# Chunked attention into a two-layer feed-forward block: VectorE's half of a step emitted one step later, squares of batch 0 moved to GpSimd, and first-layer matmuls pulled into the attention's tail

## The chip, the cores and the metric

The kernel runs on one core of a Trainium2 chip. The metric is device time in microseconds (us) of one execution, lower is better. The kernel before took 244.06 us as the median of 8 runs, 242.99 to 246.07.

## The reference

Four batches, eight heads, 768 rows, head size 64. Attention runs in chunks of 32 rows; each chunk sees 8 memory rows, 16 rows to the left of it and 8 to the right. The heads' outputs, side by side, are the 512 columns of `x`, and a feed-forward block with a sine in the middle follows (`alpha` is one number for each of 2048 hidden columns):

```python
scores = scale * np.matmul(q_c, k_full.transpose(0, 1, 3, 2))
a = np.exp(scores - max); a = a / (np.sum(a, axis=-1, keepdims=True) + 1e-09)
out[:, :, c_start:c_end] = np.matmul(a, v_full)
...
h = x @ w_in                             # 3072 x 512 by 512 x 2048
s = np.sin(alpha * h)
g = h + s * s / (alpha + 1e-09)
return (g @ w_out).astype(np.float32)    # 3072 x 2048 by 2048 x 512
```

## The kernel before, in words

All five engines run their own instructions in the order in which the program emits them (`manual_schedule`); no scheduler reorders them. What sets the order of the work is therefore the order of the code, and an engine that waits holds up everything behind it in its queue.

**Per batch** the kernel does four things.

- *Transposes.* Eight "pieces" (`t_k`, `t_q`; four pairs of heads, key and query). A piece copies heads together into `pr` (L226, VectorE, ScalarE or GpSimd), transposes it on TensorE (L242 for keys, L257 for queries) into a PSUM tile `tt`, and copies that out: keys to `kTi` on VectorE (L243 and two small L249), queries to `qT` on ScalarE (L258).
- *Attention* (`burst`), in 8 blocks of 96 rows: scores `sc` (L266), three Exp on ScalarE (L275), P·V into `ot` (L288), reciprocal and scaling on VectorE (L292, L293), transposes (L306), and a copy of `x` transposed to `xT` on VectorE (L309). In batch 0, `spin` (L171) adds matmuls on zeros.
- *First layer* (`l1`), 16 steps (`ft` 0 to 15). A step is 8 matmuls into `hT`, 128 x 2 x 384 in two PSUM banks (L341), one sine on ScalarE (`u`, L353), the square of the sine (`s2`; on ScalarE L356, on VectorE or GpSimd L358, as the string at L460 says with A, D or P), and one VectorE instruction that scales, adds `hT` and writes `gT` (L367). In batch 0, steps 3, 7 and 11 use the two small PSUM banks (`hs`) instead, with two half-width sines (L350) and two half-width VectorE instructions (L363).
- *Second layer* (`l2`), six times 16 matmuls into `o` (L393), a copy to `o_sb` (L400 on VectorE, L402 on ScalarE in turn) and a store (L403). It is a generator; `Stream.take(n)` emits its next n matmuls as filler between the steps of the following batch. If a block of 16 ends within a take, its `o_sb` copy is emitted there, and the take stops.

**PSUM**: `big` holds three tiles of two banks (`sc`, `ot`, `hT`, and `tt_b` in part), `smp` two of one bank (`o`, `z`, `hs`, `xtp`, and `tt_a`). A step's matmuls thus need the `hT` tile of three steps before, which L367 has to have read. In batches 1 and 2, one piece is emitted before every even step, and its `tt_a` shares the two small banks with `o`.

**Order around the change.** In a step of batches 1 to 3 the code emits: `take` (filler; perhaps an `o_sb` copy), a piece at even steps, then `l1` with matmuls, sine, square and L367. So on VectorE, L367 of one step stands ahead of the `o_sb` and `kTi` copies of the next.

**Loads** of weights, keys, queries and values go through GpSimd's DMA queue (L102 to L151, L212, L218); GpSimd issues them in order, and each waits for the load eight places ahead of it, whose semaphore it takes over. For batch 0's first layer the order is: 8 pieces of `w_in` (256 columns each, two steps' worth), keys and queries of batch 1, 4 pieces of `w_out` (four steps' worth each), and 4 loads of values for batch 1. The memory values of all batches are cast once on ScalarE (`memv_st`, L413), and broadcast per batch by VectorE (`put_memv`, L153).

Of the kernel before, what the change touches and what calls it, by code (L numbers as in the profile page):

```python
# [9 lines left out]
P = 128  # L10
QW = 96
# [34 lines left out]
def kernel(  # L46
# [12 lines left out]
    nc = tc.nc  # L59
    B, H, S, D = q.shape  # L60
# [16 lines left out]
    big = ctx.enter_context(tc.tile_pool(name="big", bufs=3, space=bass.MemoryType.PSUM))  # L77
    smp = ctx.enter_context(tc.tile_pool(name="smp", bufs=2, space=bass.MemoryType.PSUM))
# [129 lines left out]
    for pt in pts:  # L208
        nc.vector.memset(pt[:, H * QW:H * QW + 32], 0.0)

    def load_w_in(c):
        nc.gpsimd.dma_start(  # L212
            w_in_sb[:, :, 256 * c:256 * c + 256],
            moe_w_in[:, 256 * c:256 * c + 256].rearrange("(kt p) f -> p kt f", p=P),
        )
# [84 lines left out]
    def xt(xT, j, x_blk, ot):  # L300
        if ot is None:
            xtp = smp.tile([P, KT, QW], BF, name="xtp", tag="sm")[:]
        else:
            xtp = ot[:].bitcast(BF)[:, 0, 640:640 + KT * QW].rearrange("p (k c) -> p k c", k=KT)
        for kt in range(KT):
            nc.tensor.transpose(  # L306
                xtp[:, kt, :], x_blk[:, 2 * kt:2 * kt + 2, :].rearrange("p e d -> p (e d)"), ident[0:QW, 0:QW]
            )
        nc.vector.tensor_copy(xT[:, :, QW * j:QW * j + QW], xtp)  # L309

    def burst(b, stream, shares, lag):
# [21 lines left out]
    def l1(i, ft, xT, gT, sq, split=False):  # L333
        if split:
            hts = [smp.tile([P, 512], F32, name="hs", tag="sm") for _ in range(2)]
        else:
            hT = big.tile([P, 2, 512], F32, name="hT", tag="big")
            hts = [hT[:, 0], hT[:, 1]]
        for kt in range(KT):
            for hf in range(2):  # L340
                nc.tensor.matmul(  # L341
                    hts[hf][:, 0:HALF],
                    w_in_sb[:, kt, P * ft:P * ft + P],
                    xT[:, kt, HALF * hf:HALF * hf + HALF],
                    start=(kt == 0), stop=(kt == KT - 1),
                )
        u = mlp.tile([P, 2, HALF], F32, name="u")
        if split:
            for hf in range(2):
                nc.scalar.activation(  # L350
                    u[:, hf], hts[hf][:, 0:HALF], ACTF.Sin, scale=alpha_sb[:, ft:ft + 1])
        else:
            nc.scalar.activation(u[:], hT[:, :, 0:HALF], ACTF.Sin, scale=alpha_sb[:, ft:ft + 1])  # L353
        s2 = mlp.tile([P, 2, HALF], F32, name="s2")
        if sq == "A":
            nc.scalar.activation(s2[:], u[:], ACTF.Square)  # L356
        else:
            (nc.vector if sq == "D" else nc.gpsimd).tensor_tensor(  # L358
                out=s2[:], in0=u[:], in1=u[:], op=ALU.mult)
        gv = gT[:, ft, :].rearrange("p (e c) -> p e c", e=2)  # L360
        for hf in range(2):
            if split:
                nc.vector.scalar_tensor_tensor(  # L363
                    out=gv[:, hf], in0=s2[:, hf], scalar=inv_alpha[:, ft:ft + 1],
                    in1=hts[hf][:, 0:HALF], op0=ALU.mult, op1=ALU.add)
            elif hf == 0:
                nc.vector.scalar_tensor_tensor(  # L367
                    out=gv, in0=s2[:], scalar=inv_alpha[:, ft:ft + 1],
                    in1=hT[:, :, 0:HALF], op0=ALU.mult, op1=ALU.add)
# [39 lines left out]
    for n in range(2 * HP):  # L409
        (t_k if n % 2 == 0 else t_q)(prs[n], n // 2)  # L410
        spin(2)
        if n == 3:
            nc.scalar.copy(memv_st[64:72], memv_f[64:72])  # L413
# [105 lines left out]
```

## Time and profile before

| | |
|---|---|
| median of 8 runs | 244.06 us |
| the profiled execution | 243.94 us |
| its span, first to last instruction | 241.7 us |
| TensorE busy | 217.2 us (90%) |
| VectorE busy | 161.0 us (67%) |
| ScalarE busy | 154.6 us (64%) |
| GpSimd busy | 73.4 us (30%) |
| granted TensorE clock | 1.000 |

The stages, by the first and last instruction of each on TensorE: attention of batch 0 to 27.8 us; its first layer to 51.6; transposes of batch 1 to 61.7; attention of batch 1 to 80.3; first layer 1 to 112.5; attention 2 to 134.1; first layer 2 to 167.3; attention 3 to 189.2; first layer 3 to 217.2; and the last second layer to the end.

How to read the rows that follow: a row of a timeline has the start and the length in us, the engine, the line, the operation, what it writes and reads, and how many instructions were merged; in brackets stands how long the engine was idle before and what ended that. Engines: PE is TensorE (PEld its weight loads), DVE VectorE, ACT ScalarE, POOL GpSimd, SP the queue of the stores. A row of the waits has who waited for whom, then the total in us, how often, and the longest. TensorE's lengths include the drain of the array, so rows overlap: eight first-layer matmuls follow each other in 1.30 us.

### The profile page before, as it was taken

Reading aid. Unit: us, or ns where it says so; the run is one execution under the profiler, and the core shown is the slowest. Engines: PE = TensorE matmul, PEld = TensorE weight load, DVE = VectorE, ACT = ScalarE, POOL = GpSimd, SP = SyncE. Lnnn points to the kernel's source line nnn. Section 1 sums busy time; section 2 is a strip of 40 time slices with the busy share of each in tenths; the row PEclk is TensorE's granted clock in tenths of the full one; section 3 lists DMA queues with packets and bytes.
Section 4 is the critical chain, followed back from the end, with each engine's and each line's share of the span. In section 5 each row is a group of like instructions: output and inputs, shape, how many; then the busy total and the mean of one; then the engine's idle time right before and its main releaser. Section 6 shows DMA issues by size and latency. Waiting matters only on the chain.

```text
span 241.7 us, 4472 instructions
## 1 busy us (share of the span) xinstructions
PE 217.2 (90%) x1759; PEld 121.7 (50%) x1785; DVE 161.0 (67%) x287; ACT 154.6 (64%) x237; POOL 73.4 (30%) x96
## 2 busy tenths in 40 slices
PE   6688899978989989898999996998999999899994
PEld 2346465535445555454455653554455555453453
DVE  3578979999268667969557686968557267876100
ACT  3599499963884467788564775778764775871000
POOL 8899855423912114147210214120000001020000
PEclk9999999999999999999999999999999999999999
DMA  7999999999999810109994101001111101101122
GB/s 81 164 118 88 150 189 204 207 205 136 180 216 152 86 46 0 44 1 160 164 148 88 46 0 43 3 0 43 46 43 47 43 0 46 43 0 43 43 90 87
DMA packets 53852, 21.11 MB, mean 87 GB/s; under 512 B 36296, under 2 KB 50888, under 8 KB 53832
## 3 DMA queue, kind: packets, MB, share of 16 engines
q0 software_dynamic: 47616, 14.40, 70.1%
q1 hardware_dynamic: 6216, 6.43, 9.0%
q8 instruction: 14, 0.23, 0.4%
q14 instruction: 6, 0.05, 0.1%
HBM read 28.91 MB, written 6.29 MB: 146 GB/s over the span
## 4 chain that ended last, share of the span: by engine, by line
PE 43%; DMA 15%; DVE 13%; issue 11%; POOL 9%; ACT 7%; POOLq 1%; DVEq 0%; ACTq 0%
PE o L393 25%; DMA w_out_sb<-in_moe_w_out_dram 8%; PE hT L341 8%; DVE gT L367 6%; DVE s L358 4%; DMA w_in_sb<-in_moe_w_in_dram 4%; POOL vw L129 3%; ACT u L353 3%; PE ot L288 3%; POOL s L358 2%; PE sc L266 2%; DMA q_bf<-in_q_dram 2%; POOL vw L125 2%; ACT s L356 2%; ACT pt L275 2%
## 5 line engine op out<-in xcount | busy, mean ns | idle before, releaser
L393 PE MATMUL o<-w_out_sb,gT 128*128 128x512 bf16 x343 | 93.4, 380 | 2.8 <-DMA w_out_sb<-in_moe_w_out_dram 0.8
L341 PE MATMUL hT<-xT,w_in_sb 128*128 128x384 bf16 x488 | 87.5, 326 | 4.5 <-DVE gT L367 4.1
L367 DVE SCALAR_TENSOR_TENSOR gT<-s,inv_alpha,hT 128x768 bf16<-128x768 f32 x61 | 61.2, 1012 | 28.5 <-ACT s L356 20.0
L353 ACT ACTIVATE u<-hT,alpha_sb 128x768 f32<-128x768 f32 x61 | 54.7, 898 | 27.2 <-PE hT L341 26.0
L341 PEld LDWEIGHTS <-w_in_sb 128*128 128x128 bf16 x512 | 49.3, 98 | 39.3 <-issue 6.4
L275 ACT ACTIVATE pt<-sc,biasm 128x256 bf16<-128x256 f32 x96 | 37.6, 493 | 13.0 <-PE sc L266 13.0
L393 PEld LDWEIGHTS <-gT 128*128 128x128 bf16 x368 | 31.8, 98 | 26.4 <-DVE gT L367 1.4
L358 POOL TENSOR_TENSOR s<-u 128x768 f32<-128x768 f32 x6 | 8.8, 1466 | 73.7 <-ACT u L353 73.7
L356 ACT ACTIVATE s<-u 128x768 f32<-128x768 f32 x34 | 28.7, 843 | 1.1
L358 DVE TENSOR_TENSOR s<-u 128x768 f32<-128x768 f32 x24 | 25.2, 1049 | 0.4 <-ACT u L353 0.3
L226 POOL COPY pr<-q_bf 128x768 bf16<-128x768 bf16 x12 | 10.8, 901 | 40.0 <-PE tt_a L242 25.2
L293 DVE TENSOR_TENSOR x_blk<-ot,rinv 96x512 bf16<-96x512 f32 x32 | 22.0, 686 | 1.1
L292 DVE RECIPROCAL rinv<-ot 96x8 f32<-96x8 f32 x32 | 6.4, 201 | 20.1 <-PE ot L288 19.8
L402 ACT COPY o_sb<-o 128x512 f32<-128x512 f32 x11 | 6.4, 586 | 20.0 <-PE o L393 20.0
L400 DVE COPY o_sb<-o 128x512 f32<-128x512 f32 x12 | 8.3, 689 | 15.9 <-PE o L393 15.9
L288 PEld LDWEIGHTS <-pt 128*128 128x128 bf16 x256 | 11.9, 97 | 7.2 <-issue 2.3
L288 PE MATMUL ot<-vw,pt 128*128 128x65 bf16 x256 | 13.0, 193 | 0.9 <-ACT pt L275 0.6
L171 PE MATMUL z<-zeros 128*128 128x512 bf16 x36 | 12.5, 426 | 1.5 <-DVE zeros L165 1.3
L266 PEld LDWEIGHTS <-kTi 64*128 64x128 bf16 x256 | 6.9, 94 | 12.8 <-issue 6.4
L257 PEld LDWEIGHTS <-pr 128*128 128x128 bf16 x96 | 6.3, 97 | 13.7 <-issue 7.8
L266 PE MATMUL sc<-qT,kTi 64*128 64x96 bf16 x256 | 11.3, 205 | 1.8 <-ACT pt L275 1.2
L306 PEld LDWEIGHTS <-x_blk 96*128 96x128 bf16 x128 | 8.4, 97 | 6.6 <-DVE x_blk L293 1.5
(66 smaller groups left out, 180.8 us busy)
## 6 DMA issues: line engine op xcount, KB each, us to landing
out_dram<-o_sb SPq DMA_DIRECT2D x23, 256.0 KB, 2.2
k_bf<-in_k_dram POOLq DMA_DIRECT2D x3, 768.0 KB, 9.1
q_bf<-in_q_dram POOLq DMA_DIRECT2D x3, 768.0 KB, 12.8
vw<-in_v_dram POOLq DMA_DIRECT2D x6, 384.0 KB, 17.1
w_in_sb<-in_moe_w_in_dram POOLq DMA_DIRECT2D x8, 256.0 KB, 8.7
w_out_sb<-in_moe_w_out_dram POOLq DMA_DIRECT2D x4, 512.0 KB, 18.5
k_bf<-in_k_dram POOLq DMA_DIRECT2D x4, 192.0 KB, 5.7
q_bf<-in_q_dram POOLq DMA_DIRECT2D x4, 192.0 KB, 6.0
```

Source lines behind the costliest of these rows:

```text
L171: nc.tensor.matmul(z[:], zeros[:, 0:P], zeros[:])
L226: (eng or nc.gpsimd.tensor_copy)(pr[:].rearrange("p r e d -> p e r d"), src[:, 2 * hp:2 * hp + 2])
L266: nc.tensor.matmul(sc[:, e, QW * hp:QW * hp + QW], kTi[64 * e:64 * e + 64, hp, 104 * j:104 * j + P], qT[64 * e:64 * e + 64, hp, QW * j:QW ...
L275: nc.scalar.activation(pt[:, 0:H * QW].rearrange("p (g e c) -> p e g c", g=4, e=2)[:, :, :, 32 * m:32 * m + 32], sc[:, :, 0:4 * QW].rearra ...
L288: nc.tensor.matmul(otv[:, h // 4, h % 4, :], pt[:, QW * h:QW * h + P], vws[b % 2][:, h, j, 0:D + 1])
L293: nc.vector.tensor_tensor(out=x_blk[:].rearrange("p (g e) d -> p g e d", g=2), in0=otv[0:QW, :, :, 0:D], in1=rv.unsqueeze(3).to_broadcast( ...
L341: nc.tensor.matmul(hts[hf][:, 0:HALF], w_in_sb[:, kt, P * ft:P * ft + P], xT[:, kt, HALF * hf:HALF * hf + HALF], start=(kt == 0), stop=(kt ...
L353: nc.scalar.activation(u[:], hT[:, :, 0:HALF], ACTF.Sin, scale=alpha_sb[:, ft:ft + 1])
L356: nc.scalar.activation(s2[:], u[:], ACTF.Square)
L358: (nc.vector if sq == "D" else nc.gpsimd).tensor_tensor(out=s2[:], in0=u[:], in1=u[:], op=ALU.mult)
L367: nc.vector.scalar_tensor_tensor(out=gv, in0=s2[:], scalar=inv_alpha[:, ft:ft + 1], in1=hT[:, :, 0:HALF], op0=ALU.mult, op1=ALU.add)
L393: nc.tensor.matmul(o[:], gT[:, ft, P * s:P * s + P], w_out_sb[:, ft, :], start=(ft == 0), stop=(ft == FT - 1),)
```

## The change

It has five parts.

1. **The lag.** `l1` now returns a function `finish` with VectorE's part of the step (a square marked D, L372, and L380, which was L367; halves L376). It is called after the next step's `take` and piece, and before the next step's matmuls.
2. **Batch 0's squares**: the string goes from 10 A and 6 D to 8 A, 4 D and 4 P (steps 6, 8, 10 and 12 on GpSimd).
3. **Batch 0's attention tail**: the last three copies to `xT` go to ScalarE; the first-half matmuls (columns 0 to 383) of steps 0 and 1 are emitted at the last-but-one turn of the burst, behind P·V of block 7 and behind the transposes of block 6; the cast of `memv_st` does batch 0 at its old place and the other three batches after the burst.
4. **Fewer weight loads**: `w_in` in 5 (256, 256, 512, 512, 512 columns) instead of 8, `w_out` in 2 instead of 4.
5. **Last batch**: 2 instead of 3 second-layer matmuls per step.

```diff
-    def load_w_in(c):
+    def load_w_in(c0, c1):
...
-            w_out_sb[:, 4 * c:4 * c + 4, :],
+            w_out_sb[:, 8 * c:8 * c + 8, :],
...
-        nc.vector.tensor_copy(xT[:, :, QW * j:QW * j + QW], xtp)
+        (nc.scalar.copy if ot is None and j >= 5 else nc.vector.tensor_copy)(
+            xT[:, :, QW * j:QW * j + QW], xtp)
...
+            if hook:
+                hook(s, 0, xT)
             stream.take((n + 1) // 3, True)
             if 0 <= s - lag - 1 < NJ:
                 xt(xT, s - lag - 1, *xbl.pop(s - lag - 1))
+            if hook:
+                hook(s, 1, xT)
...
+    def l1_mm(hts, ft, xT, kt, hf):
+        nc.tensor.matmul(
+            hts[hf][:, 0:HALF],
+            w_in_sb[:, kt, P * ft:P * ft + P],
+            xT[:, kt, HALF * hf:HALF * hf + HALF],
+            start=(kt == 0), stop=(kt == KT - 1),
+        )
...
+        elif sq == "P":
+            nc.gpsimd.tensor_tensor(out=s2[:], in0=u[:], in1=u[:], op=ALU.mult)
+
+        def finish():
+            if sq == "D":
+                nc.vector.tensor_tensor(out=s2[:], in0=u[:], in1=u[:], op=ALU.mult)
...
+                elif hf == 0:
+                    nc.vector.scalar_tensor_tensor(
+                        out=gv, in0=s2[:], scalar=inv_alpha[:, ft:ft + 1],
+                        in1=hT[:, :, 0:HALF], op0=ALU.mult, op1=ALU.add)
+
+        return finish
...
-            nc.scalar.copy(memv_st[64:72], memv_f[64:72])
+            nc.scalar.copy(memv_st[64:72, 0], memv_f[64:72, 0])
...
-    for c in range(8):
-        load_w_in(c)
+    for c0, c1 in ((0, 256), (256, 512), (512, 1024), (1024, 1536), (1536, 2048)):
+        load_w_in(c0, c1)
...
+    def early(s, point, xT):
+
+        ft = {(9, 0): 0, (9, 1): 1}.get((s, point))
+        if ft is not None:
+            opened[ft] = l1_open(ft)
+            for kt in range(KT):
+                l1_mm(opened[ft], ft, xT, kt, 0)
+
+    xT = burst(0, stream, (), 2, early)
+    nc.scalar.copy(memv_st[64:72, 1:B], memv_f[64:72, 1:B])
...
-            sq = ("ADADADAAADADADAA" if i == 0 else "ADAAPDADADAPADAD")[ft]
+            sq = ("ADADAAPDPAPAPDAA" if i == 0 else "ADAAPDADADAPADAD")[ft]
             if 1 <= ft:
-                stream.take(3 if last else 2)
+                stream.take(2)
...
+            if finish is not None:
+                finish()
+            split = i == 0 and ft in (3, 7, 11)
+            if ft in opened:
+                finish = l1(ft, xT, gT, sq, opened.pop(ft), (1,))
+            else:
+                finish = l1(ft, xT, gT, sq, l1_open(ft, split), (0, 1), split)
+        finish()
```

Where this moves instructions. ScalarE, from the last Exp of batch 0's attention to the first square, before:

```order
L275 ACTIVATE pt_94<-sc,biasm 128x2x4x32 x3
L353 ACT_TABLE_LOAD
L353 ACTIVATE u<-hT,alpha_sb 128x768
L356 ACTIVATE s_619<-u 128x768
L353 ACTIVATE u<-hT,alpha_sb 128x768 x2
```

and now:

```order
L275 ACTIVATE pt_94<-sc,biasm 128x2x4x32 x3
L309 COPY xT<-xtp 128x4x96 x3
L462 CAST memv_st<-memv_f 8x1536
L363 ACT_TABLE_LOAD
L363 ACTIVATE u<-hT,alpha_sb 128x768
L366 ACTIVATE s_620<-u 128x768
```

Three copies and the larger part of the cast have come in front of the sine's table load and the first sine. VectorE, first layer of batch 1 from its start to step 4, before:

```order
L243 COPY kTi<-tt_a 128x7x96
L249 COPY kTi<-tt_a 128x48 x2
L367 SCALAR_TENSOR_TENSOR gT<-s_1304,inv_alpha,hT 128x768
L400 COPY o_sb<-o 128x512
L358 TENSOR_TENSOR s_1322<-u 128x768
L367 SCALAR_TENSOR_TENSOR gT<-s_1322,inv_alpha,hT 128x768
L367 SCALAR_TENSOR_TENSOR gT<-s_1350,inv_alpha,hT 128x768
L367 SCALAR_TENSOR_TENSOR gT<-s_1366,inv_alpha,hT 128x768
L243 COPY kTi<-tt_a 128x7x96
L249 COPY kTi<-tt_a 128x48 x2
```

and now:

```order
L243 COPY kTi<-tt_a 128x7x96
L249 COPY kTi<-tt_a 128x48 x2
L415 COPY o_sb<-o 128x512
L380 SCALAR_TENSOR_TENSOR gT<-s_1300,inv_alpha,hT 128x768
L372 TENSOR_TENSOR s_1318<-u 128x768
L380 SCALAR_TENSOR_TENSOR gT<-s_1318,inv_alpha,hT 128x768
L380 SCALAR_TENSOR_TENSOR gT<-s_1346,inv_alpha,hT 128x768
L243 COPY kTi<-tt_a 128x7x96
L249 COPY kTi<-tt_a 128x48 x2
L380 SCALAR_TENSOR_TENSOR gT<-s_1362,inv_alpha,hT 128x768
```

The copy to `o_sb` has moved ahead of step 0's L380, and the key copies ahead of step 3's. GpSimd, from the first piece of `w_in` to its first own work, before:

```order
L212 DMA w_in_sb<-in_moe_w_in_dram 128x4x256 x8
L115 DMA k_bf<-in_k_dram 128x8x384
L115 DMA q_bf<-in_q_dram 128x8x384
L218 DMA w_out_sb<-in_moe_w_out_dram 128x4x512 x4
L139 DMA vw_86<-in_v_dram 48x64x64
L142 DMA vw_86<-in_v_dram 48x64x64
L145 DMA vw_86<-in_v_dram 16x63x64
L148 DMA vw_86<-in_v_dram 8x63x64
L226 COPY pr<-q_bf 128x2x6x64 x4
```

and now:

```order
L212 DMA w_in_sb<-in_moe_w_in_dram 128x4x256 x2
L212 DMA w_in_sb<-in_moe_w_in_dram 128x4x512 x3
L115 DMA k_bf<-in_k_dram 128x8x384
L115 DMA q_bf<-in_q_dram 128x8x384
L218 DMA w_out_sb<-in_moe_w_out_dram 128x8x512 x2
L139 DMA vw_86<-in_v_dram 48x64x64
L142 DMA vw_86<-in_v_dram 48x64x64
L145 DMA vw_86<-in_v_dram 16x63x64
L148 DMA vw_86<-in_v_dram 8x63x64
L368 TENSOR_TENSOR s_702<-u 128x768
L368 TENSOR_TENSOR s_733<-u 128x768
L368 TENSOR_TENSOR s_761<-u 128x768
```

Thirteen loads stand there instead of eighteen, and behind them the squares of steps 6, 8 and 10 (and, further on, 12) ahead of the query copies.

More of the change, by code (lines that the diff above doesn't have):

```diff
@@ L209 @@
         nc.vector.memset(pt[:, H * QW:H * QW + 32], 0.0)
-    def load_w_in(c):
+    def load_w_in(c0, c1):
         nc.gpsimd.dma_start(
-            w_in_sb[:, :, 256 * c:256 * c + 256],
-            moe_w_in[:, 256 * c:256 * c + 256].rearrange("(kt p) f -> p kt f", p=P),
+            w_in_sb[:, :, c0:c1],
+            moe_w_in[:, c0:c1].rearrange("(kt p) f -> p kt f", p=P),
         )
@@ L308, in xt, with burst @@
             )
[L309 to L311 removed]
+        (nc.scalar.copy if ot is None and j >= 5 else nc.vector.tensor_copy)(
+            xT[:, :, QW * j:QW * j + QW], xtp)
+    def burst(b, stream, shares, lag, hook=None):
         xT = xp.tile([P, KT, S], BF, name="xT")
@@ L328, in burst, with l1_open, l1 @@
                 xt(xT, s - lag - 1, *xbl.pop(s - lag - 1))
+            if hook:
+                hook(s, 1, xT)
             stream.take((n + 2) // 3, True)
         return xT
-    def l1(i, ft, xT, gT, sq, split=False):
+    def l1_open(ft, split=False):
         if split:
[L335 to L338, printed above, removed]
-        for kt in range(KT):
[L340 to L346, printed above, removed]
+            return [smp.tile([P, 512], F32, name="hs", tag="sm") for _ in range(2)]
+        hT = big.tile([P, 2, 512], F32, name="hT", tag="big")
+        return [hT[:, 0], hT[:, 1], hT]
+    def l1_mm(hts, ft, xT, kt, hf):
[5 more added lines that the diff above has]
+        )
+    def l1(ft, xT, gT, sq, hts, halves, split=False):
+        for kt in range(KT):
+            for hf in halves:
+                l1_mm(hts, ft, xT, kt, hf)
+        hT = None if split else hts[2]
         u = mlp.tile([P, 2, HALF], F32, name="u")
@@ L356, in l1 @@
             nc.scalar.activation(s2[:], u[:], ACTF.Square)
[L357 to L369, printed above, removed]
+        elif sq == "P":
[3 more added lines that the diff above has]
+                nc.vector.tensor_tensor(out=s2[:], in0=u[:], in1=u[:], op=ALU.mult)
+            gv = gT[:, ft, :].rearrange("p (e c) -> p e c", e=2)
+            for hf in range(2):
+                if split:
+                    nc.vector.scalar_tensor_tensor(
+                        out=gv[:, hf], in0=s2[:, hf], scalar=inv_alpha[:, ft:ft + 1],
+                        in1=hts[hf][:, 0:HALF], op0=ALU.mult, op1=ALU.add)
+                elif hf == 0:
+                    nc.vector.scalar_tensor_tensor(
+                        out=gv, in0=s2[:], scalar=inv_alpha[:, ft:ft + 1],
+                        in1=hT[:, :, 0:HALF], op0=ALU.mult, op1=ALU.add)
+        return finish
     def l2(i, gT, last=False):
@@ L427 @@
     nc.vector.reciprocal(inv_alpha[:], alpha_sb[:])
-    for c in range(8):
-        load_w_in(c)
+    for c0, c1 in ((0, 256), (256, 512), (512, 1024), (1024, 1536), (1536, 2048)):
+        load_w_in(c0, c1)
     kq_next = load_qk(1)
-    for c in range(4):
+    for c in range(2):
         load_w_out(c)
```

6 lines of the change are left out of this document (3 added, 3 removed).

## The prediction

> **What bounds the kernel now.** I began with the busy time in the three stages that the change touches most: batch 0's first layer, then the first layers of batches 1 and 2 (columns: span, then busy time of PE, PEld, DVE, ACT, POOL).
>
> ```profile
> 27.80:51.60 23.80, 21.47 (x132) 12.47 (x129) 21.41 (x27) 20.35 (x27) 11.15 (x12) 1.00 1.32 196
> 80.30:112.50 32.20, 28.25 (x193) 16.91 (x194) 24.60 (x34) 23.72 (x29) 12.03 (x12) 1.00 0.21 39
> 134.10:167.30 33.20, 29.75 (x202) 17.48 (x205) 24.91 (x33) 23.55 (x29) 7.12 (x7) 1.00 0.07 25
> ```
>
> Batch 0 has three engines near their limit at once: VectorE 21.4 and ScalarE 20.4 of 23.8 us. In batches 1 and 2 only TensorE is full, and the granted clock is 1.00. What TensorE does not use there is what can be won. So the second view is TensorE's waits, for batches 1, 2 and 3 in turn:
>
> ```profile
> PE tt_a L257 <- DVE o_sb L400: 1.4, 1, 1.4
> PE hT L341 <- DVE gT L367: 1.0, 2, 0.5
> PE tt_a L257 <- DVE kTi L249: 1.0, 1, 1.0
> PE sc L266 <- DVE gT L367: 0.5, 1, 0.5
> ```
>
> ```profile
> PE tt_a L257 <- DVE o_sb L400: 1.7, 1, 1.7
> PE tt_a L257 <- DVE kTi L249: 1.4, 2, 0.9
> ```
>
> ```profile
> PE hT L341 <- DVE gT L367: 1.1, 2, 0.9
> PE o L393 <- DVE gT L367: 0.4, 1, 0.4
> ```
>
> That is 3.9, 3.1 and 1.5 us, every one of them on VectorE. The largest, in batch 2, row by row (GpSimd, VectorE, TensorE):
>
> ```profile
> 144.54 1.46 POOL L358 TENSOR_TENSOR s<-u 128x768 f32<-128x768 f32 x1 [5.16 <-ACT u L353]
> ```
>
> ```profile
> 146.03 1.01 DVE L367 SCALAR_TENSOR_TENSOR gT<-s,inv_alpha,hT 128x768 bf16<-128x768 f32 x1 [0.73 <-POOL s L358]
> 146.96 0.68 DVE L400 COPY o_sb<-o 128x512 f32<-128x512 f32 x1
> 147.56 0.95 DVE L358 TENSOR_TENSOR s<-u 128x768 f32<-128x768 f32 x1
> ```
>
> ```profile
> 147.70 0.49 PE L257 MATMUL tt_a<-ident,pr 128*128 128x128 bf16 x6 [1.73 <-DVE o_sb L400]
> ```
>
> VectorE stood idle 0.73 us in front of L367, for GpSimd's square. The evacuation L400 was queued behind it, and TensorE waited 1.73 us for the bank that L400 frees. It is waiting in line, not work.
>
> **The lag, batches 1 and 2.** `finish` puts L400, L243 and L249 ahead of the square and L367 of the step before. In the case shown the copy would run ahead of L367 and end before TensorE asks for the bank, so the 1.73 goes; likewise the other waits on `o_sb` and `kTi`, 1.4 + 1.0 and 1.7 + 1.4 = 5.5 us in all. The price is that L367, which frees the `hT` bank, comes after a key evacuation:
>
> ```profile
> 163.00 0.85 DVE L243 COPY kTi<-tt_a 128x672 bf16<-128x672 bf16 x1
> 163.77 0.31 DVE L249 COPY kTi<-tt_a 128x48 bf16<-128x48 bf16 x2
> ```
>
> ```profile
> 25.08 1.28 ACT L353 ACT_TABLE_LOAD   x1
> 29.73 0.90 ACT L353 ACTIVATE u<-hT,alpha_sb 128x768 f32<-128x768 f32 x1 [3.36 <-PE hT L341]
> 30.66 0.84 ACT L356 ACTIVATE s<-u 128x768 f32<-128x768 f32 x1
> 31.41 0.88 ACT L353 ACTIVATE u<-hT,alpha_sb 128x768 f32<-128x768 f32 x1
> ```
>
> ```profile
> 189.21 1.30 PE hT L341 x8
> ```
>
> A step's bank is needed again three steps on. With two second-layer matmuls (0.43) in each step and the transposes (0.34) in every second, that is two steps of 1.73 plus 0.77 = 4.2 us after its own matmuls end. Sine 0.90, square 0.84 to 0.95, L367 1.01 and handovers take 3.0. So 1.2 us is to spare, and one evacuation costs 0.85 + 0.31 = 1.16. It just fits. I charge 0.1 for each of the four key pieces: batch 2 gains 3.1 - 0.4 = 2.7. In batch 1 the second-layer matmuls run out after step 9; from there the loop is two steps of 1.30 plus 0.34 = 2.9, which is under 3.0, so half of the 1.5 us of waits for L367 (`hT` and `sc`) stays: 3.9 - 0.4 - 0.8 = 2.7. Bounds for the two together: none of it (the waits move to `hT`) up to all 7.0.
>
> **Last batch, two instead of three matmuls per step.** 26 second-layer matmuls are left there. At three a step they are gone by step 9, and the tail runs at 1.30 a step, where the 0.9 and 0.27 of waits lie. At two a step they last to step 13 at 1.73 a step, so those 1.1 us go. Against it: the last two steps are still bare (0.1), and the last `o_sb` copy on ScalarE falls in front of the last sines (I take 0.2 of its 0.6). Together -0.8; bounds 0 and -1.5.
>
> **Batch 0, when the first sine starts.** Rows of the end of its attention, of the first `w_in` piece and of the `memv_st` cast:
>
> ```profile
> 25.87 0.40 PE L288 MATMUL ot<-vw,pt 128*128 128x65 bf16 x8
> 26.50 0.34 PE L306 MATMUL xtp<-ident,x_blk 96*128 96x96 bf16 x4 [0.22 <-DVE x_blk L293]
> ```
>
> ```profile
> 22.34 5.98 POOL L212 DMA_DIRECT2D w_in_sb<-in_moe_w_in_dram  x8
> ```
>
> ```profile
> w_in_sb<-in_moe_w_in_dram POOLq DMA_DIRECT2D x1, 256.0 KB, 4.3
> ```
>
> ```profile
> 12.30 1.90 ACT L413 CAST memv_st<-memv_f 8x2048 bf16<-8x2048 f32 x1
> ```
>
> ```profile
> 27.46 0.34 DVE L309 COPY xT<-xtp 128x384 bf16<-128x384 bf16 x1
> ```
>
> ```profile
> 28.49 1.76 DVE L153 COPY vw<-memv_st 8x4096 bf16<-8x4096 bf16 x1
> ```
>
> The early matmuls stand in TensorE's queue behind 25.87 + 0.40 = 26.27 and need the first `w_in` piece, which lands at 22.34 + 4.3 = 26.64. So TensorE, which today goes straight on, waits 0.4 with the transposes of blocks 6 and 7 behind it. Then four matmuls (half of 1.30) to 27.3, transposes to 27.6, four matmuls to 28.3, the filler 0.2, and the last transposes to 28.8. ScalarE's copy of the last block: between VectorE's 0.34 and the 0.84 that ScalarE's square of twice the columns takes, I take 0.5, to 29.3. Then, new in this place, three quarters of the cast: 1.4, to 30.7. Then the table load, which before was hidden behind the attention's end: 1.28, to 32.0. The first sine was at 29.73, so ScalarE starts 2.3 us later. L153 on VectorE, which waits for the cast, runs from 30.7 to 32.5 and is covered: VectorE has nothing else until the first square ends at 33.7. The eight early matmuls win nothing, since TensorE does not hold up ScalarE here. VectorE's three copies (0.34 each) and the split of the cast win nothing either: the first cast at 12.30 only delays query copies that wait for their load anyway.
>
> **Batch 0, squares on GpSimd.** By the rows of 29.73 to 31.41 a sine with a ScalarE square takes 1.68, a sine alone 0.92. With 8 squares instead of 10, ScalarE alone would be through at 32.0 + 8 x 1.68 + 8 x 0.92 = 52.8. But a GpSimd square takes 1.46 against 0.84, and VectorE stands in line for it. Followed step by step: sine 6 ends at 41.5, its square at 43.0, while VectorE has been free since 41.7. The square of step 8 runs from 43.4 to 44.9 and meets VectorE's square of step 7. What that costs is in batch 1:
>
> ```profile
> 94.46 0.82 POOL L226 COPY pr<-k_bf 128x768 bf16<-128x768 bf16 x1
> 94.71 1.38 DVE L358 TENSOR_TENSOR s<-u 128x768 f32<-128x768 f32 x1
> ```
>
> VectorE's square took 1.38 instead of 0.95 and ended 0.81 after GpSimd's copy ended: it hardly ran beside it. So step 7's square ends at 45.7, its two L376 at 46.9. Only then can step 11 use both small banks, so its sine starts at 48.1. Sine 12 ends at 50.8, its GpSimd square at 52.4, its L380 at 53.4; step 15's matmuls need that bank and end at 54.75; sine, square and L380 end at 57.8. Against before:
>
> ```profile
> 52.71 1.93 DVE L367 SCALAR_TENSOR_TENSOR gT<-s,inv_alpha,hT 128x768 bf16<-128x768 f32 x2
> 54.56 0.85 DVE L243 COPY kTi<-tt_b 128x672 bf16<-128x672 bf16 x1
> ```
>
> ```profile
> 56.45 0.38 PE L393 MATMUL o<-w_out_sb,gT 128*128 128x512 bf16 x1 [0.77 <-DMA w_out_sb<-in_moe_w_out_dram]
> ```
>
> There L367 ended at 54.6, so VectorE reaches batch 1's key copies 3.1 us later. Part comes back: the wait of 0.77 for `w_out` is behind by then. Batch 0: +2.3. Bounds: -0.4 (VectorE starts 2.3 later, saves two squares of 0.95, never waits for GpSimd, and the 0.77 goes) and +3.4 (nothing comes back, ScalarE's copies at 0.84).
>
> Here a page bears on it: the Trainium skill, "SBUF — State Buffer", section "Who interferes with whom", says that a VectorE instruction with two SBUF inputs and a GpSimd instruction that reads SBUF exclude each other, the second waiting for the whole of the first. It speaks against putting squares on both engines in turn. The row at 94.71 agrees with it, ending 0.81 after GpSimd. If the two merely slowed each other in proportion, step 7 would lose 0.4 instead of 0.8, and the sum would be 0.4 lower.
>
> **Fewer weight DMAs.** The bytes and their order on the queue stay. Halved `w_out` means that step 8 of the second layer, not step 12, needs the last piece. It landed at 56.4; TensorE now comes to step 8 at 57.6, so it is covered. If batch 0 were not late, TensorE would wait there from 54.5, up to 1.9 us. For GpSimd the gain is needed by its squares. Before, it was held by the loads until here:
>
> ```profile
> 46.42 0.83 POOL L148 DMA_DIRECT2D vw<-in_v_dram  x1 [3.13 <-DMA q_bf<-in_q_dram]
> 47.25 1.59 POOL L226 COPY pr<-q_bf 128x768 bf16<-128x768 bf16 x1
> ```
>
> ```profile
> vw<-in_v_dram POOLq DMA_DIRECT2D x1, 63.0 KB, 18.8
> ```
>
> Each load waits for the one eight places ahead of it; with 13 loads instead of 18 the last `v` waits for the last `w_in` piece, not for `q`. All `w_in` pieces were issued by 28.3 and are ahead of `k` and `q` in the queue, so I take GpSimd as free at about 39, before its first square at 41.5. The last `v` landed at 46.42 + 18.8 = 65.2, and batch 1's first P·V needs it; 2 us later it no longer matters, but it keeps batch 0 from gaining more than about half a microsecond.
>
> **The sum.** The profiled execution took 243.94 us (span 241.7); the median of the eight is 244.06, 0.1 above. 243.94 + 2.3 - 2.7 - 2.7 - 0.8 = 240.0; against the median 240.1.
>
> **Rivals.**
> 1. Batch 0 comes out even: the later sine is made good by fewer squares on ScalarE and VectorE. For it: both are at 86 to 90% there. Against: the chain through steps 6, 8, 11, 12 and 15. 240.1 - 2.3 = 237.8. Chance 0.15.
> 2. Half of the lag's 5.4 us comes back as waits for `hT`, since 1.2 us of slack against 1.16 leaves nothing for a square held up by GpSimd: 240.1 + 2.7 = 242.8. Chance 0.18, half of it on either side of 0.5%.
> 3. Slower: GpSimd is still issuing loads when its first square is due. The row at 46.42 shows it held to 47.25; from 41.5 on every microsecond counts one for one, up to 5.7. Against: the lanes above. 240.1 + 5.7 = 245.8. Chance 0.06.
> 4. Slower: each of eight key pieces holds back L380 by its full 1.16, with TensorE waiting on `hT`: 240.1 + 5.4 - 5.5 + 9.3 = 249.3. Decides where the slack is under zero; against it is the 4.2 us. Chance 0.06.
>
> **How the numbers follow.** My forecast has 0.55, as 238.4 to 241.8. 0.5% (1.2 us) is about what a measurement can tell from no change. Faster: 0.55 + 0.15 + 0.09 = 0.79; within: 0.09; slower: 0.12. The range reaches from below rival 1 (237.0) to just over rival 2 (243.2), leaving out rivals 3 and 4 and the ends.
>
> **What would show it.** Right: first sine near 32.0; VectorE's square of step 7 about 1.7 long or late; first Exp of batch 1 (63.24 before, below) about 2.3 later; no `o_sb` or `kTi` wait of TensorE in batches 1 and 2, and those stages 2.7 us shorter; the last batch without the 0.9 wait.
>
> ```profile
> 63.24 1.20 ACT L275 ACTIVATE pt<-sc,biasm 128x256 bf16<-128x256 f32 x3
> ```
>
> Wrong: first Exp at or before 63.24 (rival 1), new waits of `hT` on L380 of over 1 us a batch (2, 4), GpSimd's first square well after 42 (3).

## The result, and the profile after

The changed kernel takes **239.09 us** (median of 11 runs, 238.07 to 240.33). The ratio to the kernel before, from the fast runs of both in one set, is 0.9764, with a 95% interval of 0.9735 to 0.9794, so it is 2.4% faster; against the 244.06 above, which is from other runs, it is 5.0 us or 2.0%. The forecast was 240.1, with a range of 237.0 to 243.2. The profiled execution took 238.53 us, with a span of 236.7 (before 243.94 and 241.7).

The quickest way to cut both spans into stages is ScalarE's table loads, which mark each change between Exp and sine. Before (L275 loads for Exp, L353 for sine; the first row is the 24 Exp of batch 0's attention, which end at 25.06):

```profile
16.13 8.93 ACT L275 ACTIVATE pt<-sc,biasm 128x256 bf16<-128x256 f32 x24 [0.37 <-PE sc L266]
...
61.95 1.28 ACT L275 ACT_TABLE_LOAD   x1
77.54 1.28 ACT L353 ACT_TABLE_LOAD   x1
112.97 1.28 ACT L275 ACT_TABLE_LOAD   x1
133.45 1.28 ACT L353 ACT_TABLE_LOAD   x1
168.71 1.28 ACT L275 ACT_TABLE_LOAD   x1
188.38 1.28 ACT L353 ACT_TABLE_LOAD   x1
```

After (sine is L363 now):

```profile
16.63 8.92 ACT L275 ACTIVATE pt<-sc,biasm 128x256 bf16<-128x256 f32 x24 [0.37 <-PE sc L266]
...
64.86 1.28 ACT L275 ACT_TABLE_LOAD   x1
80.45 1.28 ACT L363 ACT_TABLE_LOAD   x1
113.37 1.28 ACT L275 ACT_TABLE_LOAD   x1
133.05 1.28 ACT L363 ACT_TABLE_LOAD   x1
164.57 1.28 ACT L275 ACT_TABLE_LOAD   x1
184.47 1.28 ACT L363 ACT_TABLE_LOAD   x1
```

| stage | before | after | difference |
|---|---|---|---|
| start to the last Exp of batch 0 (untouched but for a shorter cast) | 25.06 | 25.55 | +0.5 |
| from there to batch 1's load for Exp (first layer of batch 0, transposes) | 36.89 | 39.31 | +2.4 |
| attention of batch 1, to the load for sine | 15.59 | 15.59 | 0 |
| from there to batch 3's load for sine (first layers of batches 1 and 2, attentions of 2 and 3) | 110.84 | 104.02 | -6.8 |
| from there to the end of the span | 53.3 | 52.2 | -1.1 |

So the gain lies where the lag acts, the last batch adds a little, and batch 0 gives back a third; e1 and e2 below take the lag apart from the rest. TensorE's share in the two lagged stages (columns: span, busy PE, PEld, DVE, ACT, POOL, then granted clock, DMA share and GB/s), each taken from batch 1's or 2's first matmul of the first layer to that of the next batch. Before:

```profile
80.69:134.46 53.77, 49.42 (x421) 28.11 (x426) 38.46 (x64) 37.16 (x57) 15.48 (x16) 1.00 0.83 77
134.46:189.05 54.59, 50.73 (x422) 28.29 (x427) 38.06 (x62) 37.23 (x58) 7.12 (x7) 1.00 0.08 29
```

After:

```profile
83.60:134.05 50.45, 49.12 (x421) 28.24 (x426) 38.87 (x64) 36.78 (x57) 15.42 (x16) 1.00 0.81 81
134.05:185.13 51.08, 49.96 (x421) 28.60 (x427) 38.02 (x62) 36.79 (x58) 7.01 (x7) 1.00 0.08 31
```

TensorE stood idle 4.35 and 3.86 us before, 1.33 and 1.12 after. What is left of its waits on VectorE, in batches 1, 2 and 3 in turn:

```profile
PE hT L345 <- DVE gT L380: 0.7, 2, 0.5
...
PE sc L266 <- DVE gT L380: 0.6, 1, 0.6
...
PE o L408 <- DVE gT L380: 0.4, 1, 0.4
```

The waits on `o_sb` and `kTi` are all gone, as forecast, and so is the 0.9 in the last batch.

The head of batch 0's first layer, on ScalarE: three copies, the cast, then the table load, which is followed by the first sine:

```profile
26.28 0.48 ACT L309 COPY xT<-xtp 128x384 bf16<-128x384 bf16 x1 [0.72 <-PE xtp L306]
27.76 0.48 ACT L309 COPY xT<-xtp 128x384 bf16<-128x384 bf16 x1 [1.00 <-PE xtp L306]
28.80 0.48 ACT L309 COPY xT<-xtp 128x384 bf16<-128x384 bf16 x1 [0.56 <-PE xtp L306]
29.30 1.47 ACT L462 CAST memv_st<-memv_f 8x1536 bf16<-8x1536 f32 x1
30.79 1.28 ACT L363 ACT_TABLE_LOAD   x1
32.09 0.90 ACT L363 ACTIVATE u<-hT,alpha_sb 128x768 f32<-128x768 f32 x1
```

And the place where squares of both engines meet, VectorE first, then GpSimd:

```profile
42.97 1.01 DVE L380 SCALAR_TENSOR_TENSOR gT<-s,inv_alpha,hT 128x768 bf16<-128x768 f32 x1 [1.26 <-POOL s L368]
43.90 1.97 DVE L372 TENSOR_TENSOR s<-u 128x768 f32<-128x768 f32 x1
45.91 1.14 DVE L376 SCALAR_TENSOR_TENSOR gT<-s,inv_alpha,hs 128x384 bf16<-128x384 f32 x2
...
43.59 1.47 POOL L368 TENSOR_TENSOR s<-u 128x768 f32<-128x768 f32 x1 [0.65 <-ACT u L363]
```

VectorE waits for GpSimd's square of step 6 (1.26), then its own square of step 7 takes 1.97 and ends 0.81 after GpSimd's.

### The profile page after: what moved, and what is told of

The parts are those of the page before. It is cut to its first block, busy times and chain, and to the rows that moved or that the text cites. A ratio compares the mean times of both kernels' runs of the same rounds, so it can differ in the third digit from the quotient of the medians.

```text
span 236.7 us, 4468 instructions
## 1 busy us (share of the span) xinstructions
PE 217.0 (92%) x1759; PEld 122.3 (52%) x1785; DVE 158.7 (67%) x282; ACT 154.1 (65%) x239; POOL 74.8 (32%) x95
## 3 DMA queue, kind: packets, MB, share of 16 engines
HBM read 28.91 MB, written 6.29 MB: 149 GB/s over the span
## 4 chain that ended last, share of the span: by engine, by line
PE 62%; ACT 12%; DVE 11%; issue 7%; POOL 3%; DMA 3%; POOLq 1%; DVEq 0%; ACTq 0%
PE o L408 29%; PE hT L345 21%; DVE gT L380 5%; ACT pt L275 4%; ACT u L363 4%; PE ot L288 3%; DMA q_bf<-in_q_dram 3%; PE sc L266 3%; DVE s L372 2%; POOL s L368 2%; ACT s L366 2%; PE ot L306 2%; PE o L397 1%; DVE x_blk L293 1%; PE tt_a L257 1%
## 5 line engine op out<-in xcount | busy, mean ns | idle before, releaser
L345 PE MATMUL hT<-xT,w_in_sb 128*128 128x384 bf16 x488 | 87.9, 326 | 5.2 <-DVE gT L380 4.5
L380 DVE SCALAR_TENSOR_TENSOR gT<-s,inv_alpha,hT 128x768 bf16<-128x768 f32 x61 | 60.8, 1013 | 22.4 <-ACT s L366 12.5
L345 PEld LDWEIGHTS <-w_in_sb 128*128 128x128 bf16 x512 | 49.3, 98 | 42.0 <-issue 8.3
L363 ACT ACTIVATE u<-hT,alpha_sb 128x768 f32<-128x768 f32 x61 | 54.8, 899 | 22.3 <-PE hT L345 22.2
L275 ACT ACTIVATE pt<-sc,biasm 128x256 bf16<-128x256 f32 x96 | 37.6, 493 | 12.5 <-PE sc L266 12.4
L368 POOL TENSOR_TENSOR s<-u 128x768 f32<-128x768 f32 x10 | 14.6, 1465 | 79.0 <-ACT u L363 66.5
L366 ACT ACTIVATE s<-u 128x768 f32<-128x768 f32 x32 | 27.0, 843 | 1.0
L372 DVE TENSOR_TENSOR s<-u 128x768 f32<-128x768 f32 x22 | 23.9, 1086 | 0.5 <-ACT u L363 0.5
L226 POOL COPY pr<-q_bf 128x768 bf16<-128x768 bf16 x12 | 10.0, 836 | 38.1 <-PE tt_a L242 26.0
L171 PE MATMUL z<-zeros 128*128 128x512 bf16 x36 | 13.2, 451 | 1.3 <-DVE zeros L165 1.3
L309 DVE COPY xT<-ot 128x384 bf16<-128x384 bf16 x24 | 8.3, 345 | 2.0 <-PE ot L306 2.0
```

Of the source, the lines that this page charges most:

```text
L275: nc.scalar.activation(pt[:, 0:H * QW].rearrange("p (g e c) -> p e g c", g=4, e=2)[:, :, :, 32 * m:32 * m + 32], sc[:, :, 0:4 * QW].rearra ...
L345: nc.tensor.matmul(hts[hf][:, 0:HALF], w_in_sb[:, kt, P * ft:P * ft + P], xT[:, kt, HALF * hf:HALF * hf + HALF], start=(kt == 0), stop=(kt ...
L368: nc.gpsimd.tensor_tensor(out=s2[:], in0=u[:], in1=u[:], op=ALU.mult)
L372: nc.vector.tensor_tensor(out=s2[:], in0=u[:], in1=u[:], op=ALU.mult)
L380: nc.vector.scalar_tensor_tensor(out=gv, in0=s2[:], scalar=inv_alpha[:, ft:ft + 1], in1=hT[:, :, 0:HALF], op0=ALU.mult, op1=ALU.add)
```

## The experiments

The theory after the result: the lag is worth 6.8 us and the two matmuls a step 1.1; batch 0's edits are a loss of 2.4 to 2.9, made of the late first sine and of GpSimd's squares. The rivals: those edits are needed for the lag's gain, or what they lose would be lost anyway. Twelve more kernels were run, each beside the kernel before (medians of 244.1 to 244.4). A ratio is to those runs and no quotient of two medians in the table; that of the changed kernel is to a set with a median of 245.0. The table has all of them, with the stages as above (from the last Exp of batch 0; the first sine counted from there too):

| run | median us | ratio and interval | to first sine | to Exp load | batches 1, 2 | end |
|---|---|---|---|---|---|---|
| before | 244.06 | 1 | 4.67 | 36.89 | 110.84 | 53.3 |
| after | 239.09 | 0.9764 (0.9735 to 0.9794) | 6.54 | 39.31 | 104.02 | 52.2 |
| e1 lag alone | 237.02 | 0.9702 (0.9651 to 0.9753) | 5.65 | 37.92 | 104.01 | 53.3 |
| e2 after, no lag, three at a time | 247.70 | 1.0124 (1.0085 to 1.0162) | 6.66 | 39.43 | 112.51 | 53.3 |
| e3 after, cast early | 236.72 | 0.9674 (0.9636 to 0.9712) | 4.91 | 36.66 | 104.02 | 52.3 |
| e4 after, old loads | 243.91 | 0.9964 (0.9934 to 0.9995) | 6.40 | 46.47 | 104.01 | 52.2 |
| e5 after, old squares | 237.67 | 0.9714 (0.9669 to 0.9758) | 6.41 | 37.42 | 104.01 | 52.2 |
| e6 e3, copies on VectorE | 237.41 | 0.9701 (0.9655 to 0.9747) | 4.58 | 37.35 | 104.00 | 52.2 |
| e7 e6, no early matmuls | 237.85 | 0.9714 (0.9670 to 0.9758) | 4.67 | 37.44 | 104.01 | 52.3 |
| e8 cast in the transposes | 238.91 | 0.9764 (0.9716 to 0.9812) | 4.59 | 39.25 | 104.01 | 52.2 |
| e9 lag and two at a time | **235.83** | 0.9646 (0.9606 to 0.9686) | 4.67 | 36.27 | 104.01 | 52.2 |
| e10 e9, new loads | 236.41 | 0.9672 (0.9637 to 0.9707) | 4.66 | 37.24 | 104.01 | 52.2 |
| e11 after, step 8 on ScalarE | 237.42 | 0.9717 (0.9680 to 0.9754) | 6.40 | 38.09 | 104.01 | 52.2 |
| e12 e10, early matmuls | 236.35 | 0.9674 (0.9635 to 0.9713) | 4.59 | 36.27 | 104.01 | 52.2 |

The stage of batches 1 and 2 has 104.0 wherever the lag is, whatever batch 0 does. The time before batch 0's last Exp differs from execution to execution (25.06 to 27.27), so medians differ by a little more or less than the stages.

**e1_lag_only**: the changed kernel with all but the lag taken back.

```diff
-            sq = ("ADADAAPDPAPAPDAA" if i == 0 else "ADAAPDADADAPADAD")[ft]
+            sq = ("ADADADAAADADADAA" if i == 0 else "ADAAPDADADAPADAD")[ft]
-                stream.take(2)
+                stream.take(3 if last else 2)
-    xT = burst(0, stream, (), 2, early)
-    nc.scalar.copy(memv_st[64:72, 1:B], memv_f[64:72, 1:B])
+    xT = burst(0, stream, (), 2)
...
```

> The kernel before with the lag alone (finish called one step late in all four batches); everything else as before. Theory, from the stages of the two profiles: batch 0 costs 2.9 us in the changed kernel and the lag wins 3.2 in batch 1 and 3.6 in batch 2, so the lag alone gives 244.1 - 6.8 = about 237.3, and the first sine is back at 29.7. First rival: the lag is worth the 5.4 that the prediction gave it, and the other 1.4 come from the other edits of the changed kernel (the loads, the squares): 238.7. Second rival: what batch 0 loses is partly given back behind it, so without that loss the lag finds less to win: 239 to 240.

237.02: the theory. Both rivals, 238.7 and 239 or more, are out, and the lag alone wins the same 6.8 in its stage. By the medians it does better than the whole change; the two intervals still overlap a little, and e9 below, with two matmuls a step added, is clear of it. (This profile's first sine is about 1 us late for another reason, told at the end.)

**e2_no_lag_123**: the other half alone.

```diff
-            if finish is not None:
+            if finish is not None and i == 0:
                 finish()
...
+            if i > 0:
+                finish()
-        finish()
+        if i == 0:
+            finish()
```

> The changed kernel with finish called at once in batches 1 to 3, and three second-layer matmuls per step in the last batch: only the edits of batch 0 and of the loads are left. Theory: 244.1 + 2.9 = 247.0, the first Exp of batch 1 at 66.1, TensorE's waits for o_sb and kTi back. Rival: what batch 0 loses is absorbed later where the lag isn't there, 244 to 245.5.

247.70, so nothing is absorbed: without lag and with three at a time the change is 1.2% slower than before. (The stage of batches 1 and 2 is 1.67 longer than before's in this profile, for a reason told at the end.) TensorE's waits on `o_sb` and `kTi` in batch 1 and then 2 are back, to the tenth:

```profile
PE tt_a L257 <- DVE o_sb L415: 1.4, 1, 1.4
PE tt_a L257 <- DVE kTi L249: 1.0, 1, 1.0
...
PE tt_a L257 <- DVE o_sb L415: 1.7, 1, 1.7
PE tt_a L257 <- DVE kTi L249: 1.4, 2, 0.9
```

**e3_cast_early**:

```diff
-            nc.scalar.copy(memv_st[64:72, 0], memv_f[64:72, 0])
+            nc.scalar.copy(memv_st[64:72], memv_f[64:72])
...
-    nc.scalar.copy(memv_st[64:72, 1:B], memv_f[64:72, 1:B])
```

> The changed kernel with the whole cast of memv_st at its old place, in the prologue. Theory: the 1.47 us of cast ahead of the sine's table load go straight on to the end of batch 0: first sine at 30.6, first Exp of batch 1 about 64.7, time 1.4 below the changed kernel, 237.7. Rival: the chain through GpSimd's squares and the small banks sets the end of batch 0 whenever the first sine comes: first sine at 30.6, first Exp still at about 66, 239.1.

236.72, more than the 1.4 expected. From the last Exp the first sine comes 1.63 sooner. Of that 1.49 is the cast: e4, e5 and e11, which have it in the changed kernel's place, need 6.40 to 6.41. The other 0.13 is a wait for `w_in`: the first early matmul starts 0.36 behind the start of the last P·V in the changed kernel, 0.24 in those three and in e3. Another 1.0 comes behind the first sine in this profile, from the meeting of the squares. VectorE, then GpSimd:

```profile
43.99 0.95 DVE L372 TENSOR_TENSOR s<-u 128x768 f32<-128x768 f32 x1
...
43.98 2.29 POOL L368 TENSOR_TENSOR s<-u 128x768 f32<-128x768 f32 x1 [0.96 <-ACT u L363]
```

Here the two start 0.01 apart, VectorE runs through in 0.95, and GpSimd's square takes 2.29 instead of 1.47. In the changed kernel GpSimd was 0.31 ahead, and VectorE paid. From the first start to the last end it is 2.28 and 2.29 us, nearly 0.95 + 1.47 = 2.42, so the two hardly overlap. The Trainium skill, "SBUF — State Buffer", section "Who interferes with whom", has it that the order of issue decides who blocks, and that the second waits for the first's whole instruction; that one of the two waits, the rows show: 1.97 and 2.29 against 0.95 and 1.47 alone. Who was issued first they do not show in e3, where GpSimd's row even starts 0.01 ahead and yet VectorE's runs through. Which engine pays matters: when it is GpSimd, the stage behind the first sine is 31.75 instead of 32.77. How often it falls out so is open: of the runs at a mean granted clock of 0.998 or more, the changed kernel's have a median of 238.28 and e3's 236.81, which is 1.5 apart, the cast alone.

**e4_old_loads**:

```diff
-    for c0, c1 in ((0, 256), (256, 512), (512, 1024), (1024, 1536), (1536, 2048)):
-        load_w_in(c0, c1)
+    for c in range(8):
+        load_w_in(256 * c, 256 * c + 256)
...
-    for c in range(2):
+    for c in range(4):
         load_w_out(c)
```

> The changed kernel with the weights loaded as before, 8 pieces of w_in and 4 of w_out. Third rival of the prediction: GpSimd is still issuing loads when its first square is due, at 41.5; it comes free near 46.4, and the first square starts near 47, up to 5.7 us late: 242 to 245. Theory that the loads were only bundled: the first square starts within 1 us of 41.5, and the time stays at 239.1.

243.91, 2% slower than the changed kernel: the third rival's mechanism is real, and the bundled loads are what kept it off. GpSimd, then ScalarE, then TensorE's waits in batch 0:

```profile
46.94 0.83 POOL L148 DMA_DIRECT2D vw<-in_v_dram  x1 [3.13 <-DMA q_bf<-in_q_dram]
47.80 2.90 POOL L368 TENSOR_TENSOR s<-u 128x768 f32<-128x768 f32 x2
...
49.31 0.90 ACT L363 ACTIVATE u<-hT,alpha_sb 128x768 f32<-128x768 f32 x1 [5.99 <-POOL s L368]
```

```profile
PE hT L345 <- DVE gT L380: 10.2, 4, 6.8
```

The first GpSimd square starts at 47.80 behind the last load instead of at 41.48, and every engine waits for it. The wait has a second price: by single microseconds, TensorE's granted clock is 0.50 from 49 to 55, and in all twelve runs its mean is only 0.977 to 0.993. So the time lost is not the late square alone.

**e5_old_squares**: batch 0's string as before, all else as changed.

```diff
-            sq = ("ADADAAPDPAPAPDAA" if i == 0 else "ADAAPDADADAPADAD")[ft]
+            sq = ("ADADADAAADADADAA" if i == 0 else "ADAAPDADADAPADAD")[ft]
```

> The changed kernel with batch 0's squares as before (10 on ScalarE, 6 on VectorE, none on GpSimd). The first sine stays at 32.1. Theory: the squares on GpSimd cost about what they save, and the late first sine is the loss; the first layer then runs as before, 2.4 later, and batch 1's table load for Exp comes at 64.0 instead of 64.86: 238.3. Rival: the chain through steps 6, 8, 11 and 12 is a loss of its own beside the late sine, above 1 us: 237.5 or less. Second rival: fewer squares on ScalarE are a gain that the collisions hide: 240 or more.

237.67, between the theory (238.3) and the first rival (237.5 or less). The stage decides: from the first sine to the Exp load 31.01, against 32.77 with GpSimd's squares, so they cost 1.76 behind a late sine. The first rival's mechanism holds: they are a loss of their own.

**e11_no_square_at_8** separates the meeting at steps 7 and 8:

```diff
-            sq = ("ADADAAPDPAPAPDAA" if i == 0 else "ADAAPDADADAPADAD")[ft]
+            sq = ("ADADAAPDAAPAPDAA" if i == 0 else "ADAAPDADADAPADAD")[ft]
```

> The changed kernel with the square of step 8 of batch 0 on ScalarE instead of GpSimd, so that VectorE's square of step 7 has no GpSimd square beside it. Theory: the two engines' squares exclude each other, VectorE's takes 0.95 instead of 1.97, and the first layer of batch 0 ends 1.0 earlier: first Exp's table load 31.75 after the first sine instead of 32.77, 238.1. Rival: ScalarE's extra 0.84 takes its place: 239.1.

```profile
31.89 0.90 ACT L363 ACTIVATE u<-hT,alpha_sb 128x768 f32<-128x768 f32 x1
...
63.58 1.28 ACT L275 ACT_TABLE_LOAD   x1
...
43.70 0.95 DVE L372 TENSOR_TENSOR s<-u 128x768 f32<-128x768 f32 x1
```

The square takes 0.95 and the stage 31.69 instead of 32.77. That one meeting costs 1.08 of the 1.76 (of the runs at a mean granted clock of 0.998 or more, the medians are 238.28 and 237.12, 1.2 apart); ScalarE's additional square of 0.84 does not take its place.

**e6_cast_early_copies_vector** and **e7_also_no_early_matmuls**: e3 with

```diff
-        (nc.scalar.copy if ot is None and j >= 5 else nc.vector.tensor_copy)(
-            xT[:, :, QW * j:QW * j + QW], xtp)
+        nc.vector.tensor_copy(xT[:, :, QW * j:QW * j + QW], xtp)
```

and then also with `burst(0, stream, (), 2)`, without the hook.

> The cast as in the run before (all of it in the prologue, 236.7) and the three xT copies on VectorE again. ScalarE is then free at the last Exp, and the table load of 1.28 is hidden. Theory: from the last Exp to the first sine 4.3 us (6.5 in the changed kernel, 4.9 with the early cast alone), so 0.6 off: 236.1. Rival: TensorE's second-half matmuls hold the sine anyway, and the copies on ScalarE cost nothing: 236.7.

> The run above without the matmuls of steps 0 and 1 inside the attention's tail. Theory: with ScalarE free, TensorE sets the first sine, and four matmuls fewer behind the last xT copy are worth 0.4 us: 4.7 us from the last Exp to the first sine as in the kernel before, 236.5, so 0.4 slower than with them. Rival: they win nothing, as the prediction said: no difference.

Both medians, 237.41 and 237.85, lie above the times expected (236.1 to 236.7), and neither can be told from the run before it (236.72 for e3; the intervals overlap). By the stages, the copies on VectorE bring the first sine 0.33 nearer, but in e6's profile GpSimd's square of step 8 was first again and VectorE's took 1.97 (1.83 in e7), which hides it. The early matmuls are worth 0.09: they win nothing, as predicted.

**e8_cast_in_transposes**: the changed kernel with e6's copies, and

```diff
-    nc.scalar.copy(memv_st[64:72, 1:B], memv_f[64:72, 1:B])
     put_memk(1)
-    put_memv(1)
...
+                    if n == 2:
+                        nc.scalar.copy(memv_st[64:72, 1], memv_f[64:72, 1])
+                        put_memv(1)
+                    if n == 4:
+                        nc.scalar.copy(memv_st[64:72, 2:B], memv_f[64:72, 2:B])
```

> The changed kernel with the xT copies on VectorE and the cast in three parts: batch 0's at its old place, batch 1's and the last two batches' in ScalarE's gaps between the query copies of batch 1's transposes (1.2 to 1.5 us idle each), with VectorE's broadcast for batch 1 there too. If the full cast of 1.90 in the prologue is hidden: as with the early cast and the copies on VectorE, 236.1. If it delays the query copies of batch 0: up to 1.3 less, 234.8. If the parts in the transposes delay query copies of batch 1: 0.5 more, 236.6.

238.91, slower than all three expectations. They looked at ScalarE, but the loss is on VectorE, then TensorE:

```profile
59.49 1.80 DVE L153 COPY vw<-memv_st 8x4096 bf16<-8x4096 bf16 x1
61.33 0.69 DVE L414 COPY o_sb<-o 128x512 f32<-128x512 f32 x1
...
62.07 0.49 PE L257 MATMUL tt_a<-ident,pr 128*128 128x128 bf16 x6 [1.73 <-DVE o_sb L414]
```

The broadcast for batch 1 went in front of an `o_sb` copy, and TensorE waited 1.73 for the bank: the same waiting in line that the lag removes, put in by hand. Whether the full cast in the prologue costs anything stays open, since this run's first part says nothing on it.

**e9_lag_and_two, e10_lag_two_loads, e12_lag_two_loads_early**: e1 with `stream.take(2)` in the last batch; then with the bundled loads; then with the hook as well.

> The kernel before with the lag and with two second-layer matmuls per step in the last batch; nothing else changed. Theory: the lag alone gave 237.0, and the last stage is 1.1 shorter with two at a time (53.3 us from the last table load to the end with three, 52.2 with two): 235.9, so 3.2 below the whole change. Rival: the two gains overlap, since both act on the waits for L380 in the last batch: 237.0.

> The run above with the bundled loads of the changed kernel. Theory, as the prediction had it: with batch 0 on time, step 8 of the second layer comes at 54.5 and needs the second half of w_out, which lands at 56.4; TensorE waits up to 1.9 there instead of 0.77, so up to 1.1 slower: 236 to 237. Rival: the wait for w_out goes with the larger pieces, since GpSimd issues them earlier: 235.1.

> The second run of this call with the matmuls of steps 0 and 1 inside the attention's tail added. Theory: they win nothing, 4.6 us from the last Exp to the first sine instead of 4.7, and the same time within 0.3. Rival: TensorE holds the sine up once ScalarE is free, and they win 0.4 or more.

e9 takes 235.83, the theory's 235.9 and the best of all kernels: 3.5% under before, and under the whole change with intervals that do not touch. e10 takes 236.41, within the 236 to 237 expected, and its trace shows the wait that the prediction named for a batch 0 on time:

```profile
PE o L407 <- DMA w_out_sb<-in_moe_w_out_dram: 1.6, 1, 1.6
```

It is 0.4 in e9 and 0.9 in e12, whose attention ended 1.7 us later than e10's. The intervals of e9 and e10 overlap, but their runs at a mean granted clock of 0.998 or more do not: 235.23 to 236.07 and 236.27 to 236.87. That is 1.0 between the medians, as between the stages (36.27 and 37.24). e12's median equals e10's.

## Why the prediction was right, point by point

- **What bounds the kernel** (VectorE's line in batches 1 and 2): right. e1 and e2 show it from both sides.
- **The lag, -5.4: mis-sized, it was -6.8**, close to the bound of 7.0. In batch 1 the charge of 0.8 for waits on L380 was right (0.7 stayed), but key pieces in front of L380 cost nothing there; in batch 2 a wait of 0.6 before `sc` is new, against 0.4 charged. By the waits alone 3.2 and 2.5 go, while the stages shrink by 3.3 and 3.5. Half of the 1.0 in batch 2 that no row of the waits names is in how a wait is counted: a row's idle time begins at the modelled end of the matmul before. From start to start the three waits of before cost 1.91, 0.74 and 1.04, which is 0.5 more than their rows. Of the other half, 0.3 lies in the step from 143.78 to 145.36 of before (1.58 for eight matmuls instead of 1.30); why is open. This term makes up the miss of 1.0 against 244.06: 1.4 too small, the last batch 0.3 too small, and against them 0.1 in batch 0 and the 0.5 by which this execution's attention ended later.
- **The last batch, -0.8**: measured -1.1 (53.3 to 52.2 with nothing else changed, e1 and e9).
- **First sine at 32.0**: 32.09. The copies took 0.48 (0.5 taken), the cast 1.47 (1.4), the table load 1.28. Of the wait of 0.4 for `w_in` only 0.13 arose, since this execution's attention ended 0.5 later: the early matmuls (L345) start close behind P·V.

```profile
26.37 0.40 PE L288 MATMUL ot<-vw,pt 128*128 128x65 bf16 x8
26.73 0.82 PE L345 MATMUL hT<-xT,w_in_sb 128*128 128x384 bf16 x4
```

  So that the sine came at 32.09 is partly luck: 0.5 of scatter stood in for the rest of the wait. Counted from the last Exp, the head costs 1.87, not 2.3: 1.49 for the cast, 0.13 for the wait, 0.33 for the copies, and -0.09 for the early matmuls.
- **Squares on GpSimd**: step 7's square ended at 45.87 (45.7 predicted), its L376 at 47.05 (46.9), the last L380 at 58.1 (57.8). Taken by itself GpSimd's part costs 1.76, of which 1.08 for one meeting, where 0.8 was counted beyond VectorE's free time. The two squares nearly exclude each other (2.28 together, 2.42 one after the other), as the prediction took it.
- **What comes back, 0.77 for `w_out`**: that wait is gone, and e10 shows the other side, 1.6 (up to 1.9 predicted). But 1.2 came back: with the old squares behind the late sine (e5) the stage behind the first sine is 31.01, before 32.22. Where the other 0.4 comes from no run isolates.
- **The sum for batch 0, +2.3**: it measured +2.4 from the last Exp on, and that it fits so well is luck. The head was 0.4 less than predicted, GpSimd's squares 1.0 more, and 0.4 more came back.
- **Rival 1** (batch 0 even) is out: e9 without the edits is 3.3 faster. **Rivals 2 and 4** are out: waits for `hT` fell from 1.0 to 0.7 in batch 1, and in batch 2 there are none. **Rival 3** did not come: GpSimd was through with the loads at 38.4, near the 39 predicted. With the old loads it did come, at 4.8 between the medians, the slower clock included, where 5.7 was its bound.

## What to carry to other kernels

When TensorE waits for an evacuation, look at what stands in front of that evacuation in its engine's queue: emitting the long chain's tail one step later cost no work and won 2.8%, and one careless broadcast (e8) lost 1.7 us in the same way. A change of five parts can be a gain with a loss inside: run each part alone, since here two of the five gave all of it. Before squares go from ScalarE to GpSimd, ask whether VectorE has a square of its own at that time, and whether GpSimd is still issuing loads.

## What the runs showed of the hardware

**Who pays hangs on a few tenths of a microsecond.** In five profiles (the changed kernel, e2, e6, e7 and e8) GpSimd's square of step 8 started 0.30 to 0.46 ahead, and VectorE's took 1.83 to 1.98. In e3 the two rows start 0.01 apart, VectorE's took 0.95, and batch 0 was 1.0 shorter. That is one profile, so where the border lies is open.

**The granted clock dips for a few microseconds in some executions.** In e2, in ten microseconds of batch 2; in e1, at batch 0's first layer; and in e4, behind its long wait (the granted clock is the third number from the right):

```profile
150.00:160.00 10.00, 9.41 (x52) 5.03 (x51) 6.50 (x7) 5.51 (x7) 1.65 (x2) 0.83 0.07 26
```

```profile
30.00:40.00 10.00, 10.00 (x53) 5.53 (x52) 6.83 (x8) 7.18 (x10) 7.23 (x7) 0.83 1.39 197
```

```profile
50.00:55.00 5.00, 4.63 (x15) 2.22 (x15) 4.51 (x6) 1.95 (x3) 1.52 (x2) 0.50 1.39 199
```

By single microseconds the clock is 0.50 from 151 to 154 in e2 and from 30 to 33 in e1. A mean of 0.83 over 10 us is 3.4 us at that half speed, 1.7 lost; e2's stage is 1.67 longer than before's. e1's first sine, at 32.09, is 1 us late by the same. The runs of the changed kernel show it too: at a mean clock of 0.998 or more they took 238.07 to 238.93, at 0.993 239.1 to 239.5, at 0.986 240.3. The Trainium skill, "TensorE: Matmul & The Clock Gate", Part 1, speaks of half rate set by activity windows of about 3.4 us; the size agrees in e1 and e2. In e4 the dip begins about 5 us into a standstill of TensorE. In e1 and e2 no row shows what set it off: e2's follows a wait of 1.7 that the kernel before has without a dip.

**The prologue scatters.** In the changed kernel's profile TensorE was at full pace from its second fillers on (0.59 for two), in e3's not until 14, though the granted clock is given as 1.00 in both; the first copy of keys started at 6.00 and 6.29. After, then e3:

```profile
6.97 0.59 PE L171 MATMUL z<-zeros 128*128 128x512 bf16 x2
```

```profile
7.33 1.06 PE L171 MATMUL z<-zeros 128*128 128x512 bf16 x2
```

The last Exp of batch 0 ended at 25.55 and 27.27. So two profiles are compared from there on, and differences of under 1 us between medians of six runs are left to the stages.
